# A scan and a feed-forward layer on one core: one wide warm-up product replaced by 32 products of a single column

## The chip, the core and the metric

The kernel runs on one core of a Trainium2 chip. A core has five instruction streams: TensorE (PE in the profile, with its weight loads shown apart as PEld), VectorE (DVE), ScalarE (ACT), GpSimd (POOL) and SyncE (SP), which here only issues DMAs. They meet through semaphores. The metric is the device time of one execution in microseconds: the median of three executions of the kernel before is 309.92 us (309.73 to 310.04).

## The reference

The first half is a gated linear recurrence (a chunked scan) over 4 batches, 8 heads and 768 steps; the second is a feed-forward layer on its output.

```python
for c in range(nc):                       # chunks of the sequence
    cum = np.cumsum(la, axis=-1)          # la = log(clip(a))
    L = np.exp(cum[:, :, :, None] - cum[:, :, None, :]) * causal
    M = np.einsum('bhin,bhjn->bhij', Cc, Bc) * L
    y[:, :, sl] = M @ xc + (Cc @ state) * np.exp(cum)[..., None]
    state = decay_full * state + sum_j(Bc * xc * decay_from_j)
x = y.transpose(0, 2, 1, 3).reshape(3072, 256)
h = x @ w_in                              # 256 -> 2048
return np.maximum(0.01 * h, h) @ w_out    # 2048 -> 256
```

## The kernel before

The sequence is cut into 16 chunks of 48 steps. For each chunk PE forms the logarithms of the decay (`decay_stack`, L267, or for the first two chunks `decay_mask` and `decay_direct`, L249 and L259), ACT takes their exponent (L291), PE forms the scores of C and B (`scores`, L323), DVE multiplies both (`weigh`, L337), and PE multiplies the result with the values (`chunk_products`, L353: 32 products in float32, each of which the profile shows as two). DVE transposes the new state out of PSUM (`states`, L377), and POOL, ACT and DVE copy it in pieces of 16 partitions to where the next chunk reads it (L388). The cumulative sums that most chunks need are made once, by `sums` (L211), from the logarithms of `a`; ACT and DVE split them in three bfloat16 parts, which go through a scratch tensor in memory.

The feed-forward layer runs over tiles of 512 tokens and 16 blocks of 128 hidden features. `ffn_in` (L503) is six products of 512 columns, `ffn_out` (L527) another six; ACT and DVE split what lies between them into a high and a low part (L510, L513, L516). The weights arrive in float64 and are decoded on the way by ACT, DVE and POOL (`decode`, L426 to L472). Later tiles go in pairs through a scheme with fewer products (`two_tiles`, L771 and L796).

The order of the work is written out by hand: each engine runs its instructions in the order in which the code names them. First come constants, the sums and chunks 0 to 2, then a loop over steps, in which one block of the feed-forward layer stands between the pieces of a chunk.

Before any data has arrived, PE runs products on a tile of zeros, `idle`, whose results nobody reads. The helper is `keep_warm` (L118 to L124): each call of it makes `n` products of a 128x128 weight tile with 512 columns. At the start `n` is `WARM`; they write to the second bank of the tile `first`, whose real use begins with `sums`, later on PE's own stream. Between steps 0 and 1 of the loop four more stand (`BRIDGE`).

The lines around the change:

```python
first = banks()
keep_warm(first[:, 1], WARM)
```

Of the kernel before, what the change touches and what calls it, by code (L numbers as in the profile page):

```python
# [29 lines left out]
TS = 512  # L30
LAG = 3
OUT_AT = {1: 0, 2: 1, 3: 2, 4: 3, 5: 4, 8: 5}
WARM = 4
BRIDGE = {1: 4}
RAWS = 3
SLOTS = 2
# [27 lines left out]
def scan_ffn(ctx: ExitStack, tc: tile.TileContext, a_l, c_l, d_l, x_l, w_l, out_l):  # L64
    nc = tc.nc
# [21 lines left out]
    def banks():  # L87
        return ps_c.tile([128, 2, TS], F32, name="sc")
# [26 lines left out]
    idle = const.tile([128, 944], BF16, name="idle")  # L115
    nc.vector.memset(idle[:, :128], 0.0)

    def keep_warm(space, n):  # L118
        for _ in range(n):
            nc.tensor.matmul(  # L120
                space, lhsT=idle[:, :128],
                rhs=idle[:, :128].unsqueeze(1).to_broadcast([128, TS // 128, 128]),
                start=True, stop=True,
            )  # L124

    nc.scalar.preload_act_table_set("natural_log_exp_and_others")
    first = banks()
    keep_warm(first[:, 1], WARM)

    la = pe.tile([128, NC * NM], F32, name="la")  # L130
    nc.sync.dma_start(la, a_l)
# [603 lines left out]
    rhs = {}  # L735
# [318 lines left out]
```

## Time and profile before

| what | before |
| --- | --- |
| median of 3 executions | 309.92 us (309.73 to 310.04) |
| the profiled execution's own time | 309.52 us |
| its span, first to last instruction | 307.5 us |
| PE busy, share of the span | 297.2 us, 97% |
| DVE, ACT, POOL busy | 219.2, 181.8, 72.0 us |
| memory read and written | 20.02 and 3.44 MB |

The span begins with the first instruction and ends with the last; 2.0 us of the execution lie around it. A busy share is an average over the whole span: the first 45 us, where the scan starts up and weights are decoded, look different from the rest. In the rows of a timeline the first number is the start in us, the second the time from there to the end of the last instruction of the row, and x is how many instructions a row holds; in brackets stands how long the engine was idle before it, and what ended that.

### The profile page before, as it was taken

Reading aid. Unit: us, or ns where it says so; the run is one execution under the profiler, and the core shown is the slowest. Engines: PE = TensorE matmul, PEld = TensorE weight load, DVE = VectorE, ACT = ScalarE, POOL = GpSimd, SP = SyncE. Lnnn points to the kernel's source line nnn. Section 1 sums busy time; section 2 is a strip of 40 time slices with the busy share of each in tenths; the row PEclk is TensorE's granted clock in tenths of the full one; section 3 lists DMA queues with packets and bytes.
Section 4 is the critical chain, followed back from the end, with each engine's and each line's share of the span. In section 5 each row is a group of like instructions: output and inputs, shape, how many; then the busy total and the mean of one; then the engine's idle time right before and its main releaser. Section 6 shows DMA issues by size and latency. Waiting matters only on the chain.

```text
span 307.5 us, 6801 instructions
## 1 busy us (share of the span) xinstructions
PE 297.2 (97%) x2712; PEld 234.8 (76%) x2712; DVE 219.2 (71%) x392; ACT 181.8 (59%) x344; POOL 72.0 (23%) x154
## 2 busy tenths in 40 slices
PE   8796999999999999999999999999999999999994
PEld 4464777777777777888888888888888888888883
DVE  6778787987786679975878777776775475547552
ACT  7877566766766554755456565674565455545452
POOL 5444866866676630000000000000000000000000
PEclk9958899999999999999999999999999999999998
DMA  7777764656643101000100000000020000000003
GB/s 238 218 253 237 264 183 158 224 195 220 186 125 112 63 2 71 0 2 0 68 1 2 0 0 0 2 1 0 2 102 34 0 2 1 0 0 2 0 0 136
DMA packets 12644, 23.89 MB, mean 78 GB/s; under 512 B 4549, under 2 KB 4933, under 8 KB 12613
## 3 DMA queue, kind: packets, MB, share of 16 engines
q1 hardware_dynamic: 12612, 23.46, 23.3%
q8 instruction: 21, 0.34, 0.4%
q14 instruction: 11, 0.08, 0.1%
HBM read 20.02 MB, written 3.44 MB: 76 GB/s over the span
## 4 chain that ended last, share of the span: by engine, by line
PE 92%; DVE 3%; issue 2%; ACT 1%; POOL 0%; POOLq 0%; DVEq 0%
PE sc L771 18%; PE op L527 15%; PE op L796 14%; PE sc L796 14%; PE hp L503 14%; PE hp L771 7%; PE sc L353 4%; PE sc L323 3%; PE sc L267 2%; PE sc L120 1%; DVE top L449 1%; PE pd L353 1%; DVE lt L337 1%; DVE gl L516 0%; DVE stage L377 0%
## 5 line engine op out<-in xcount | busy, mean ns | idle before, releaser
L388 POOL COPY xs<-stage 16x128 f32<-16x128 f32 x106 | 37.5, 354 | 26.0 <-DVE stage L377 20.7
L510 ACT ACTIVATE gh<-hp 128x512 fp32r<-128x512 f32 x32 | 19.1, 598 | 28.6 <-PE hp L503 28.4
L807 ACT ACTIVATE gh<-u 128x512 fp32r<-128x512 f32 x32 | 20.0, 625 | 17.7 <-DVE u L848 17.7
L527 PE MATMUL op<-gh,wh 128*128 128x512 f32 x64 | 28.4, 444 | 0.0
L811 DVE TENSOR_TENSOR gl<-u,gh 128x512 fp32r<-128x512 f32 x32 | 22.0, 686 | 7.9 <-ACT u L808 7.9
L847 DVE TENSOR_TENSOR u<-sc,kept 128x512 f32<-128x512 f32 x16 | 11.1, 692 | 22.2 <-PE sc L771 22.2
L807 ACT ACTIVATE gh<-kept 128x512 fp32r<-128x512 f32 x16 | 10.1, 632 | 28.1 <-DVE kept L856 28.1
L527 PE MATMUL op<-gl,wh 128*128 128x512 f32 x64 | 25.6, 399 | 0.1
L527 PE MATMUL op<-gh,wl 128*128 128x512 f32 x64 | 25.5, 399 | 0.0
L807 ACT ACTIVATE gh<-hp 128x512 fp32r<-128x512 f32 x16 | 9.6, 598 | 26.8 <-PE hp L771 26.8
L856 DVE TENSOR_TENSOR kept<-sc,kept 128x512 f32<-128x512 f32 x16 | 11.1, 692 | 19.5 <-PE sc L771 19.3
L796 PE MATMUL op<-gh,wh 128*128 128x512 f32 x64 | 24.9, 389 | 0.0
L796 PE MATMUL sc<-gh,wh 128*128 128x512 f32 x64 | 24.9, 389 | 0.0
L796 PE MATMUL sc<-gh,wl 128*128 128x512 f32 x64 | 24.9, 389 | 0.0
L796 PE MATMUL op<-gh,wl 128*128 128x512 f32 x64 | 24.9, 389 | 0.0
L796 PE MATMUL op<-gl,wh 128*128 128x512 f32 x64 | 24.9, 389 | 0.0
L796 PE MATMUL sc<-gl,wh 128*128 128x512 f32 x64 | 24.9, 389 | 0.0
L337 DVE TENSOR_TENSOR lt<-sc,lt 128x384 f32<-128x384 f32 x32 | 16.3, 549 | 11.3 <-ACT gh L510 8.1
L516 DVE TENSOR_TENSOR gl<-hp,gh 128x512 fp32r<-128x512 f32 x32 | 21.6, 676 | 3.1 <-ACT hp L513 3.1
L472 POOL TENSOR_TENSOR wl<-w,wh 128x512 fp32r<-128x512 f32 x16 | 20.7, 1294 | 11.4 <-ACT wh L471 11.2
L503 PE MATMUL hp<-xh,wh 128*128 128x512 f32 x64 | 20.9, 408 | 0.0
L808 ACT ACTIVATE u<-u 128x512 f32<-128x512 f32 x32 | 20.2, 632 | 1.0
(150 smaller groups left out, 737.8 us busy)
## 6 DMA issues: line engine op xcount, KB each, us to landing
raw<-w_l SPq DMA_DIRECT2D x16, 512.0 KB, 3.8
bcn<-d_l SPq DMA_DIRECT2D x13, 448.0 KB
xs<-x_l SPq DMA_DIRECT2D x16, 256.0 KB, 3.0
out_l<-ob SPq DMA_DIRECT2D x12, 256.0 KB, 2.0
bcn<-c_l SPq DMA_DIRECT2D x3, 352.0 KB
dl<-left_d SPq DMA_DIRECT2D x14, 9.0 KB, 1.6
dr<-right_d SPq DMA_DIRECT2D x14, 9.0 KB
left_d<-parts SPq DMA_DIRECT2D x2, 72.0 KB, 2.4
```

What stands on the lines that cost most here:

```text
L337: nc.vector.tensor_tensor(out=to, in0=at, in1=to, op=ALU.mult)
L388: copy(xss[c + 1][h * R:h * R + N, 2 * p:2 * p + 2, bs], stage[rows, :, bs],)
L472: nc.gpsimd.tensor_tensor(out=wl[:, f], in0=w32s[f], in1=wh[:, f], op=ALU.subtract)
L503: nc.tensor.matmul(hp, lhsT=w_half[h][:, f, k * 128:(k + 1) * 128], rhs=x[t][:, k, :], start=(n == 0), stop=(n == 5),)
L510: nc.scalar.activation(ghs[s], hp, AF.Prelu, alpha=0.01)
L516: nc.vector.tensor_tensor(out=gls[s], in0=hps.pop(s), in1=ghs[s], op=ALU.subtract)
L527: nc.tensor.matmul(op, lhsT=w_half[h][:, f, DM + m * 128:DM + (m + 1) * 128], rhs=x, start=(start and i == 0), stop=(last and i == 2),)
L771: nc.tensor.matmul(bank, lhsT=w[h], rhs=x[g], start=start and i == 0, stop=i == 2, skip_group_check=True,)
L796: nc.tensor.matmul(outs[t][m], lhsT=w_half[h][:, f, DM + m * 128:DM + (m + 1) * 128], rhs=x, start=start and i == 0, stop=last and i == 2,)
L807: nc.scalar.activation(gh, h, AF.Prelu, alpha=0.01)
L808: nc.scalar.activation(in_place, h, AF.Prelu, alpha=0.01)
L811: nc.vector.tensor_tensor(out=gl, in0=g, in1=gh, op=ALU.subtract)
```

## The change

`WARM` goes from 4 to 3, and behind the three wide products stand 32 products of one row of weights, one column of weights and one column of data. They read the same zeros and write one element of the same bank. Nothing else is edited.

```diff
-WARM = 4
+WARM = 3
+NARROW = 32
...
     first = banks()
     keep_warm(first[:, 1], WARM)
+    for _ in range(NARROW):
+        nc.tensor.matmul(
+            first[:1, 1, :1], lhsT=idle[:1, :1], rhs=idle[:1, :1], start=True, stop=True,
+        )
```

On PE the stream before begins like this; `sc` is the bank written to, `bars` the weights of the first real products, `decay_mask`. Lines of the changed file stand five lower from there on.

```order
L1041 UNCONDITIONAL_BRANCH
L120 LDWEIGHTS idle
L120 MATMUL sc<-idle 128x512
L120 LDWEIGHTS idle
L120 MATMUL sc<-idle 128x512
L120 LDWEIGHTS idle
L120 MATMUL sc<-idle 128x512
L120 LDWEIGHTS idle
L120 MATMUL sc<-idle 128x512
L249 LDWEIGHTS bars
```

In the changed kernel PE's stream has the last of the three wide products, and then the first narrow ones, each with a weight load of its own:

```order
L121 LDWEIGHTS idle
L121 MATMUL sc<-idle 128x512
L131 LDWEIGHTS idle
L131 MATMUL sc<-idle 1x1
L131 LDWEIGHTS idle
```

and where they end, the first real products:

```order
L131 LDWEIGHTS idle
L131 MATMUL sc<-idle 1x1
L254 LDWEIGHTS bars
L254 MATMUL pd<-later,bars 128x384
```

One load and one product are gone, 32 loads and 32 products have come: from L254 on everything on PE stands 62 instructions later in its stream (1190 rows of the order, 1128 before), in the same order as before. The streams of DVE, ACT, POOL and SP hold the same instructions in the same order.

## Rows read from the trace of the kernel before

**Rows 1.** From the page: the engines' busy time and instruction counts, and the span in 40 equal slices (each 7.7 us; the busy share in tenths, and the TensorE clock that was granted, in tenths of full speed).

```profile
PE 297.2 (97%) x2712; PEld 234.8 (76%) x2712; DVE 219.2 (71%) x392; ACT 181.8 (59%) x344; POOL 72.0 (23%) x154
PE   8796999999999999999999999999999999999994
PEclk9958899999999999999999999999999999999998
```

**Rows 2.** Timeline of PE, from the start of the span to 13.4 us.

```profile
1.06 1.89 PE L120 MATMUL sc<-idle 128*128 128x512 bf16 x4 [1.06 <-DVE idle L116]
2.74 1.49 PE L249 MATMUL pd<-later,bars 112*128 112x384 bf16 x4
4.02 1.01 PE L211 MATMUL sc<-ends_at,la 112*128 112x96 f32 x4
...
6.13 0.89 PE L323 MATMUL sc<-cs,bcn 32*64 32x96 f32 x32 [0.18 <-ACT cs L302]
6.95 0.30 PE L587 MATMUL sc<-la,after 48*64 48x16 f32 x8
7.09 1.01 PE L259 MATMUL pd<-reach,after 48*64 48x384 f32 x8
8.28 0.86 PE L353 MATMUL pd<-lt,xs 64*32 64x64 f32 x64 [0.19 <-POOL lt L308]
...
10.91 1.41 PE L353 MATMUL sc<-lt,xs 64*32 64x64 f32 x51 [0.31 <-POOL xs L388]
13.09 0.34 PE L353 MATMUL sc<-lt,xs 64*32 64x64 f32 x13 [0.77 <-issue]
```

**Rows 3.** Timeline: the weight loads of L211 on PEld, and ACT's logarithms, whose results L211 reads.

```profile
3.14 0.60 ACT L568 ACTIVATE la<-la 128x32 f32<-128x32 f32 x2
...
3.81 0.29 PEld L211 LDWEIGHTS sc<-ends_at,la 112*128 112x128 f32 x1 [0.28 <-issue]
```

**Rows 4.** Timeline of PE, from 13.3 us on.

```profile
13.36 0.50 PE L267 MATMUL pd<-dr,dl 102*128 102x384 bf16 x2
13.79 0.89 PE L323 MATMUL sc<-cs,bcn 32*64 32x96 f32 x32
15.48 1.74 PE L353 MATMUL pd<-lt,xs 64*32 64x64 f32 x64 [0.80 <-POOL xs L388]
17.15 0.82 PE L267 MATMUL sc<-dr,dl 102*128 102x384 bf16 x2
17.90 0.90 PE L323 MATMUL sc<-bcn 32*64 32x96 f32 x12
19.03 1.22 PE L323 MATMUL sc<-bcn 32*64 32x96 f32 x20 [0.23 <-issue]
20.19 1.22 PE L503 MATMUL hp<-xh,wh 128*128 128x512 f32 x2
21.21 1.05 PE L503 MATMUL hp<-xl,wh 128*128 128x512 f32 x2
22.06 0.74 PE L503 MATMUL hp<-xh,wl 128*128 128x512 f32 x2
22.64 0.50 PE L267 MATMUL sc<-dr,dl 102*128 102x384 bf16 x2
22.98 1.03 PE L120 MATMUL hp<-idle 128*128 128x512 bf16 x4
23.66 0.81 PE L503 MATMUL hp<-xh,wh 128*128 128x512 f32 x2
24.31 0.62 PE L503 MATMUL hp<-xl,wh 128*128 128x512 f32 x2
24.77 0.63 PE L503 MATMUL hp<-xh,wl 128*128 128x512 f32 x2
25.34 0.86 PE L353 MATMUL sc<-lt,xs 64*32 64x64 f32 x64
26.12 0.72 PE L323 MATMUL sc<-bcn 32*64 32x96 f32 x24
29.32 0.60 PE L323 MATMUL sc<-bcn 32*64 32x96 f32 x8 [2.48 <-issue]
```

**Rows 5.** From the page: one of the DMA queues (packets, megabytes, share of the 16 engines' time).

```profile
q8 instruction: 21, 0.34, 0.4%
```

**Rows 6.** Timeline of DVE around the first of PE's stops, and of ACT and DVE after the third.

```profile
13.17 0.30 DVE L443 TENSOR_SCALAR mag<-mag 128x512 uint16<-128x512 uint16 x1
13.51 0.45 DVE L377 STREAM_TRANSPOSE stage<-sc 128x256 f32<-128x256 f32 x1
...
34.16 0.60 ACT L510 ACTIVATE gh<-hp 128x512 fp32r<-128x512 f32 x1 [2.74 <-PE hp L503]
...
36.09 0.29 DVE L438 TENSOR_SCALAR mag<-mag 128x512 bf16<-128x512 bf16 x1 [1.78 <-ACT mag L426]
```

**Rows 7.** The table of busy time by stretches: stretch, its length, busy time of PE, PEld, DVE, ACT and POOL with the number of instructions, the granted clock of TensorE, the DMA engines' share and GB/s.

```profile
15.49:18.90 3.41, 3.19 (x78) 1.89 (x78) 3.30 (x9) 3.31 (x9) 0.38 (x1) 0.50 0.79 284
18.90:22.32 3.42, 3.29 (x25) 2.68 (x26) 2.15 (x5) 1.43 (x5) 3.23 (x6) 0.50 0.72 200
22.32:25.70 3.38, 3.38 (x51) 2.06 (x51) 2.52 (x5) 3.30 (x7) 1.48 (x2) 1.00 0.62 189
25.73:29.14 3.41, 1.12 (x65) 0.90 (x55) 3.27 (x6) 2.29 (x5) 1.99 (x2) 1.00 0.95 304
29.14:32.56 3.42, 3.23 (x14) 2.45 (x14) 3.38 (x8) 1.10 (x2) 2.09 (x4) 0.50 0.77 241
```

## The prediction

> **What bounds the kernel now.** I read the slices of the page first. PE is busy in nine tenths or more of every slice but three early ones and the last, so a microsecond that PE loses before about 45 us is lost for good, unless another engine was late at that place anyway [rows 1]. Then I read PE's timeline through that early part, row by row, looking at the brackets. Two things are to be seen there.
>
> The first is the start. The four wide products run from 1.06 us, the first real ones (L249) from 2.74, so a wide one takes 1.68 / 4 = 0.42 us, and the four L249, from 2.74 to 4.02, 0.32 us each [rows 2]. 512 columns in 0.42 us and 384 in 0.32 are both 1.2 GHz, the lower of the clock's two levels. Behind them stands L211. Its weights are the logarithms, which ACT finishes at 3.14 + 0.60 = 3.74 us, and its weight load starts at 3.81 [rows 3]; its product starts at 4.02, just where the last L249 ends. So PE's own work and the logarithms come due at nearly the same time. A PE that is later than now delays L211 in full; one that is earlier gains at most 0.2 us. Everything of the scan hangs on L211, since ACT's next work reads it.
>
> The second is three places where PE is idle and the bracket names "issue": no semaphore and no engine ended the wait. They are 0.77 us inside a group of L353 after its 51st product of 64, 0.23 us inside a group of L323 after the 12th of 32, and 2.48 us inside another group of L323 after the 24th of 32 [rows 2, 4]. Nothing in the code stands at these places. Counted along PE's rows, 13 + 2 + 32 + 64 + 2 + 12 = 125 products lie between the first stop and the second, and 20 + 6 + 2 + 4 + 6 + 64 + 24 = 126 between the second and the third [rows 4]. With a weight load for each and a few semaphore waits that is about 256 instructions both times. The DMA queue q8 carried instructions: 21 packets with 0.34 MB, 16 KB each [rows 5]; PE's 2712 products and 2712 loads [rows 1] divided by 21 are 258 instructions a packet. I take the three stops for refills of PE's instruction store that came too late, one at each border of 256 instructions, in a stretch where DMAs keep their engines 62 to 95% busy [rows 7].
>
> [...]
>
> **The change part by part.** Durations are those of the profiled execution (309.52 us, span 307.5 with 2.0 around it); it lies 0.40 below the median of 309.92, and I add the sum to the median.
>
> *One wide product goes:* -0.42 us.
>
> *32 narrow ones come.* No row shows a product of one column. From below, the rows of L353 at 8.28 bound it: 64 products with 64 loads in 0.86 us, 13 ns each, or 0.43 us for 32. These lie on different parts of the array, and narrow ones all on the same. From above, a narrow one could wait for its own weight load each time; the nearest load that stands alone is L211's, 0.29 us for 128 columns in float32 [rows 3], or 9.3 us for 32. That is far off, since in L353 64 loads pass in 0.86 us. Nearer are L587, the shortest stream of data here (16 columns), with 8 in 0.30 us, 37 ns each or 1.20 us, and L323, with 32 in 0.89, 28 ns each [rows 2]. I take L323, whose count is that of the change: 0.89 us. The two parts together are +0.47 us, between 0 and +0.8 by the near rows, and it lies in full on the way to L211. The lower end is not below nothing by more than the 0.2 us that L211 could gain.
>
> [...]
>
> *The borders move.* 31 more products and 31 more loads stand ahead of everything, so each border falls 31 products earlier in the program: the first after the 20th of the 64 products of L353 (about 11.7 us on the old clock), the second after the 47th of the group of L353 at 15.48 (about 16.6), the third after the 57th of the group at 25.34 (about 26.0) [rows 2, 4]. I assume that a refill is asked for when the border before it is crossed, since the time from one restart to the next landing is what varies; that crossing is now earlier too: 11.7 in place of 13.09 for the second and 16.6 in place of 19.03 for the third. For the third, the time from one border to the next grows from 29.32 - 2.48 - 19.03 = 7.8 to 9.4 us; for the second it shrinks from 5.7 (18.80 - 13.09) to 4.9. I forecast that the stops mostly go.
>
> What that is worth: the first stop is hidden. DVE was busy until 13.17 + 0.30 = 13.47 and took its transpose at 13.51, 0.02 us after PE's last product, so PE could have been earlier for nothing [rows 6]. The second is worth its 0.23 us. The third is 2.48 us on PE; ACT waited 2.74 us for the L503 behind it, but DVE, which is busy 3.27 and 3.38 of 3.4 us in the two stretches beside it, waited only 1.78 us at 36.09 [rows 6, 7]. So DVE is next late, and 1.78 us is what comes through. Together -2.01 us.
>
> *The clock* was halved from 15.49 to 22.32 and from 29.14 to 32.56; PE was busy 1.12 us of 3.41 ahead of the second [rows 7]. Without the third stop that second stretch may be at full speed, worth up to half of its 3.23 busy us, 1.6; or PE, now waiting for DVE a little later, makes it fall later, and loses as much. I take 0 and keep both for the range.
>
> Sum: -0.42 + 0.89 - 2.01 = -1.54 us, so 309.92 - 1.54 = 308.4 us. By the ends (0 and +0.8 for the narrow ones, -1.6 for the clock) this case runs from 309.92 - 2.01 - 1.6 = 306.3 to 309.92 - 2.01 + 0.8 = 308.7, and to 309.2 if half a microsecond of stops stays.
>
> **The rivals.**
>
> *The clock rises later.* In the rows of the start PE is at 1.2 GHz; at 6.13 L323 takes 0.89 us for 32 products, the same as at full speed later, where 20 take 1.22 us at half [rows 2, 4]. So the clock rises at about 5 us, behind four microseconds of dense wide products. Now about one of these holds products that fill one cell of the array. From 15.49 to 18.90 PE was busy 3.19 of 3.41 us, mostly with products on small parts of the array, and the clock stayed at 0.50 after it [rows 7]. Against it speaks that three wide ones, L249 and L211 stay. If the clock stays low until about 10 us, a group of scores goes from 26 ns a product (6.13 to 6.95 for 32) to 58 (19.03 to 20.19 for 20), +1.0 us for 32, and a group of L353 from 0.86 to about 1.5, +0.6. Two groups of scores and one of L353 on the way make +2.6 us, and with the forecast's other terms 311.0 us. It decides from 1.5 us of added time on. [...]
>
> *The narrow ones are dear.* If load and product took turns on the one place of the array, at 0.10 us a pair (a third of L211's load alone), 32 would cost 3.2 us. Then 3.2 - 0.42 - 2.01 = +0.8, 310.7 us. Against it: loads in L353 pass at 13 ns [rows 2].
>
> *The refills take as long as before.* From crossing to restart the second took 19.03 - 13.09 = 5.9 us and the third 29.32 - 19.03 = 10.3. With these, the second lands at 11.7 + 5.9 = 17.6, a stop of 1 us in place of 0.23, and the third at 27.9, 1.4 before the old one, but with 7 products of L353 and 24 of L323 still to run, 0.8 us. The gain left is about 0.5 us and the narrow ones eat it: 309.9 us. For it speaks that a refill's time seems set by the DMAs around it; against it, that those DMAs are not the same ones at the earlier crossings.
>
> [...]
>
> **How the numbers follow.** The forecast has 0.42, the later clock 0.22, dear narrow ones 0.14, refills as slow as before 0.14, no refills 0.08. About 0.2%, 0.6 us, is what a measurement of this kernel can tell from no change: faster means under 309.3, slower over 310.5. The forecast is faster (0.42, and 0.01 from refills half as slow); slow refills and no refills fall within (0.21 of their 0.22); the two first rivals are slower, 0.36. The forecast's own range is 306.3 to 309.2; its low end needs the whole gain of the clock, so the range with both signs begins at 307.0, and it ends at 311.6, above both slower cases by half a microsecond.
>
> **What would show it.** In PE's timeline of the changed kernel the first L254 starts at 2.32 + 0.89 = 3.2 us and L216 (the old L211) at about 4.5. The "issue" brackets, if any are left, stand 31 products earlier in the program, and the waits named "issue" before the scores sum to under 1 us. The scores at about 6.6 us take 0.89 us if the clock has risen, near 1.9 if not. ACT's wait for L508 (the old L503) near 34 us is shorter than 2.74. The forecast is wrong if a stop of over 1 us stands inside a group of L358 or L328, if the first real product starts after 4 us, or if the granted clock is low at 7 us.

## The result, and the profile after

The changed kernel is slower: 311.42 us (median of 20, 309.63 to 312.68), and the kernel before, run beside it, 309.55 (20, 308.28 to 311.04). The ratio is 1.006, 95% interval 1.004 to 1.008. The forecast was 308.4.

One thing must be known to read the profile after. Its execution took 309.63 us, the shortest of the 20. A second profile of the same kernel, taken in the first experiment, took 311.35, close to the median. I call them the short and the typical execution and use both.

From the page of the short execution, the lines that answer to [rows 1] and [rows 5]:

```profile
PE 296.1 (96%) x2743; PEld 232.7 (76%) x2743; DVE 221.0 (72%) x392; ACT 181.7 (59%) x344; POOL 72.5 (24%) x154
...
PE   8978789999999999999999999999999999999994
...
PEclk9999999999999999999999999999999999999999
...
q8 instruction: 21, 0.34, 0.4%
```

31 more products, as many packets on q8 (21). PE's timeline of the short execution, the start, against [rows 2], and the places where PE waits later, against [rows 4]:

```profile
1.06 1.46 PE L121 MATMUL sc<-idle 128*128 128x512 bf16 x3 [1.06 <-DVE idle L117]
2.45 0.94 PE L131 MATMUL sc<-idle 1*1 1x1 bf16 x32
3.32 1.46 PE L254 MATMUL pd<-later,bars 112*128 112x384 bf16 x4
4.57 1.01 PE L216 MATMUL sc<-ends_at,la 112*128 112x96 f32 x4
...
7.00 1.56 PE L328 MATMUL sc<-cs,bcn 32*64 32x96 f32 x32
...
13.02 1.21 PE L358 MATMUL sc<-lt,xs 64*32 64x64 f32 x64 [0.31 <-POOL xs L393]
...
32.55 0.48 PE L272 MATMUL sc<-dr,dl 102*128 102x384 bf16 x2 [1.76 <-issue]
...
41.83 0.48 PE L272 MATMUL sc<-dr,dl 102*128 102x384 bf16 x2 [1.11 <-issue]
```

The narrow products start 25 ns apart (32 lie between 2.45 and 3.25); from the first of them to L254 it is 0.87 us, and L216 starts 0.55 us later than L211 did. The three stops inside L353 and L323 are gone. But the scores at 7.00 take 1.56 us where they took 0.89: the records of the granted clock begin, at full, only at 10.91 us, before at 5.25 (the slices of the page show the time ahead of the first record as full). And two new waits stand before L272, which the view also calls "issue"; the rows of DVE below show what is late there.

The typical execution, same view:

```profile
13.72 1.19 PE L358 MATMUL sc<-lt,xs 64*32 64x64 f32 x64 [0.32 <-DMA dl<-left_d]
...
17.47 0.78 PE L358 MATMUL pd<-lt,xs 64*32 64x64 f32 x46 [0.24 <-DVE lt L342]
19.71 0.47 PE L358 MATMUL pd<-lt,xs 64*32 64x64 f32 x16 [1.47 <-issue]
20.11 0.82 PE L272 MATMUL sc<-dr,dl 102*128 102x384 bf16 x2
20.87 1.55 PE L328 MATMUL sc<-bcn 32*64 32x96 f32 x32
22.35 1.22 PE L508 MATMUL hp<-xh,wh 128*128 128x512 f32 x2
...
34.31 0.48 PE L272 MATMUL sc<-dr,dl 102*128 102x384 bf16 x2 [1.38 <-issue]
43.59 0.48 PE L272 MATMUL sc<-dr,dl 102*128 102x384 bf16 x2 [1.10 <-issue]
```

Here the second stop is back: 1.47 us, behind the 48th of 64 products (2 + 46) of the L358 group, where the prediction's count put the border (the 47th). The table of stretches of the same execution, against [rows 7]:

```profile
18.90:22.32 3.42, 2.60 (x50) 1.62 (x50) 1.78 (x6) 2.02 (x7) 0.83 (x1) 0.57 0.15 41
25.73:29.14 3.41, 3.41 (x79) 2.24 (x77) 3.10 (x6) 2.73 (x7) 1.08 (x1) 0.93 0.73 231
```

Behind the stop the clock is down (0.57 in the mean) and the loads are through (DMA share 0.15). In the second stretch PE is busy 3.41 of 3.41 us, where the third stop had left 1.12.

**Where the time went.** Two rows of DVE cut the execution into three parts: M is the L438 (after: L443) behind its wait for ACT near 24 us, P the transpose L377 (L382) near 46. In the kernel before they are

```profile
23.62 0.97 DVE L438 TENSOR_SCALAR mag<-mag 128x512 bf16<-128x512 bf16 x1 [0.79 <-ACT mag L426]
...
46.29 0.45 DVE L377 STREAM_TRANSPOSE stage<-sc 128x256 f32<-128x256 f32 x1 [1.22 <-PE sc L353]
```

In the typical execution of the changed kernel (timeline of DVE and POOL):

```profile
25.91 1.05 DVE L443 TENSOR_SCALAR mag<-mag 128x512 bf16<-128x512 bf16 x1 [0.78 <-ACT mag L431]
...
33.22 0.98 DVE L342 TENSOR_TENSOR lt<-sc,lt 128x384 f32<-128x384 f32 x2
...
39.03 3.04 POOL L477 TENSOR_TENSOR wl<-w,wh 128x512 fp32r<-128x512 f32 x2
...
39.54 1.38 DVE L443 TENSOR_SCALAR mag<-mag 128x512 bf16<-128x512 bf16 x1
40.95 1.26 DVE L448 TENSOR_SCALAR mag<-mag 128x512 uint16<-128x512 uint16 x1
...
42.51 0.98 DVE L342 TENSOR_TENSOR lt<-sc,lt 128x384 f32<-128x384 f32 x2
...
48.06 0.45 DVE L382 STREAM_TRANSPOSE stage<-sc 128x256 f32<-128x256 f32 x1 [1.16 <-PE sc L358]
```

Both L342 end (34.20 and 43.49) 0.1 us before the L272 that waited (34.31 and 43.59): PE waits there for DVE. Up to M it loses 25.91 - 23.62 = 2.29 us. From M to P it takes 22.15 in place of 22.67, a gain of 0.52. From P to the end of the time it is 311.35 - 48.06 = 263.29 against 309.52 - 46.29 = 263.23. In all 20 profiles of this study this last part lies between 263.2 and 263.6 us. So everything is decided before P, and the loss lies ahead of M.

In the typical execution the chain that ended last leads from the second stop to M: the 1.47 us of the stop, the rest of L358, L272, the scores L328 until 22.47, then L342, L454 and L463 on DVE, L476 and L431 on ACT, and M. The start of L508, which stands behind the scores on PE, is used below as the mark of their end.

### The profile page after: what moved, and what is told of

It is laid out like the page before. It is cut to its first block, busy times and chain, and to the rows that moved or that the text cites. A ratio compares the mean times of both kernels' runs of the same rounds, so it can differ in the third digit from the quotient of the medians.

```text
span 307.6 us, 6863 instructions
## 1 busy us (share of the span) xinstructions
PE 296.1 (96%) x2743; PEld 232.7 (76%) x2743; DVE 221.0 (72%) x392; ACT 181.7 (59%) x344; POOL 72.5 (24%) x154
## 3 DMA queue, kind: packets, MB, share of 16 engines
q1 hardware_dynamic: 12612, 23.46, 23.5%
## 4 chain that ended last, share of the span: by engine, by line
PE 87%; DVE 5%; DMA 4%; SPq 1%; issue 1%; ACT 0%; DVEq 0%
PE sc L776 18%; PE op L801 14%; PE sc L801 14%; PE op L532 14%; PE hp L508 13%; PE hp L776 7%; PE sc L358 3%; PE sc L328 2%; DMA bcn<-d_l 2%; PE sc L272 1%; DMA left_d<-parts 1%; DVE top L454 1%; DVE w L463 1%; DMA dr<-right_d 1%; DVE gl L521 1%
## 5 line engine op out<-in xcount | busy, mean ns | idle before, releaser
L393 POOL COPY xs<-stage 16x128 f32<-16x128 f32 x106 | 36.9, 349 | 27.6 <-DVE stage L382 22.2
L342 DVE TENSOR_TENSOR lt<-sc,lt 128x384 f32<-128x384 f32 x32 | 16.3, 549 | 11.1 <-ACT gh L515 8.3
L477 POOL TENSOR_TENSOR wl<-w,wh 128x512 fp32r<-128x512 f32 x16 | 21.1, 1326 | 7.3 <-ACT wh L476 7.0
L508 PE MATMUL hp<-xh,wh 128*128 128x512 f32 x64 | 20.3, 398 | 0.3 <-ACT wh L476 0.3
```

What stands on the lines that cost most here:

```text
L342: nc.vector.tensor_tensor(out=to, in0=at, in1=to, op=ALU.mult)
L393: copy(xss[c + 1][h * R:h * R + N, 2 * p:2 * p + 2, bs], stage[rows, :, bs],)
L477: nc.gpsimd.tensor_tensor(out=wl[:, f], in0=w32s[f], in1=wh[:, f], op=ALU.subtract)
L508: nc.tensor.matmul(hp, lhsT=w_half[h][:, f, k * 128:(k + 1) * 128], rhs=x[t][:, k, :], start=(n == 0), stop=(n == 5),)
```

## The experiments

Ratios are to the kernel before, run beside each, with the 95% interval. Times of refills are the starts of the 16 KB packets on q8 in the trace's DMA records. "Clock" is the time from which the records grant it in full.

**The changed kernel again, and the kernel before again** (no edit).

> The changed kernel once more, for a second profile of it, since its times spread by 3 us and the profile there is one of its fastest executions. All theories: 310.5 to 312 us. Theory D (the code refill that now comes at 8.5 us holds up the save of the sums, left_d, on which SP's queue waits): left_d lands 3.5 us or more after its issue again, the refill's packet lies beside it. Theory C (the clock rises later behind the narrow products): the granted clock rises after 7 us again. Theory F (refills still come too late in most executions): stops named issue of over 1 us stand in PE's timeline 31 products earlier than before.

> The kernel before once more, for a second profile of it. Theory C: the clock rises near 5 us again. Theory R (the refill stops are part of this kernel in every execution): stops named issue inside the same three groups, after the 51st, 12th and 24th product, 2 to 4 us together; if they are shorter here, their length is set by the DMAs of one execution.

The changed kernel: 311.49, ratio 1.0085 (1.0067 to 1.0103), the typical execution above. The kernel before: 309.18, ratio 1.0014 (0.9990 to 1.0038); in its profile the clock happened to rise as late as in the changed kernel, at 13.05 us. That execution took 309.63, 0.45 over the median of its own 12 runs. PE's timeline and M and P of DVE's:

```profile
13.25 1.18 PE L353 MATMUL sc<-lt,xs 64*32 64x64 f32 x64
...
18.26 0.55 PE L323 MATMUL sc<-bcn 32*64 32x96 f32 x12
19.66 0.71 PE L323 MATMUL sc<-bcn 32*64 32x96 f32 x20 [0.85 <-issue]
20.30 0.73 PE L503 MATMUL hp<-xh,wh 128*128 128x512 f32 x2
...
23.96 1.08 DVE L438 TENSOR_SCALAR mag<-mag 128x512 bf16<-128x512 bf16 x1 [0.78 <-ACT mag L426]
...
46.34 0.45 DVE L377 STREAM_TRANSPOSE stage<-sc 128x256 f32<-128x256 f32 x1 [1.22 <-PE sc L353]
```

This is the pair to look at. Second packet at 17.35 here, 17.41 in the typical execution of the changed kernel; PE goes on at 19.66 here, 19.71 there. The refill is equally late. But here PE stands behind the 12th of 32 scores and reaches the feed-forward product 0.64 us later; there 16 products of L358, L272 and all 32 scores are still to come, 2.64 us at the half clock that follows the stop.

**The wide products alone**: `WARM = 5`, `WARM = 3`, `WARM = 0`, no narrow ones; the borders stay within ten instructions of where they were.

> Five wide products at the start and no narrow ones: PE reaches the first real product 0.43 us later, nearly what the change does (0.57), with a dense start and the refill borders where they were. If delay alone is the cause (theory L) the time rises by 0.4 us or more, towards what the change costs. Theories C and D: like the kernel before, within 0.5 us; refills, left_d and the clock's rise (near 5 us) as before.

> Three wide products and no narrow ones: the other half of the edit alone, without the moved borders. Theory C in the form that a wide product is missed: the clock rises later than before and the time goes up by 1 us or more. Theory D: the same as before, or up to 0.2 us faster, with left_d landing 2.4 us after its issue as before.

> No product before the first real ones at all: PE begins near 2.4 us. No narrow products, borders moved by 8 instructions only, and no delay. Theory C prices the late clock alone: it rises after 8.5 us, and the time is 2 to 3 us over the kernel before, about that of the change. If delay, borders or collision are the cause of the change's loss, this kernel is within 0.5 us of the kernel before.

Medians 309.73, 309.78, 309.30; ratios 1.0012 (0.9984 to 1.0039), 1.0026 (1.0002 to 1.0050), 1.0018 (0.9992 to 1.0044). The clock rose at 5.51 with five, at 12.79 with three and at 12.60 with none. Without any warm-up the kernel can't be told from the one before, and the 2 to 3 us that theory C gave for e11 are out: a late clock with the old borders costs little or nothing (only the interval of e3 stays clear of 1, by 0.0002).

**The borders moved, with the start as before.** 31 narrow products later in PE's stream, behind the four wide ones: behind the first `decay_direct` (e12) or behind the `reverse` products L597 (e4, e10, the same kernel twice).

```
+        for _ in range(31):
+            nc.tensor.matmul(
+                pd[:1, 0, :1], lhsT=idle[:1, :1], rhs=idle[:1, :1], start=True, stop=True,
+            )
         states(0, os, (0, 0, 0, 2, 0, 2, 0, 2))
```

> Four wide products as before, and 31 narrow ones behind the two products of L597, where PE waits for the copies of the state anyway. The start is that of the kernel before, but every refill border behind the first falls 31 products earlier, as in the change. Theory D: the first refill is asked for as before, left_d lands as before (2.4 us), the stops at 12, 19 and 27 us shrink, and the time is 0.5 to 2 us under the kernel before. Theory F: the moved borders are what costs, and the time is above the kernel before by 1 us or more. Theory C: as before or faster.

> e4 once more, for a second profile and more times. Theory C: clock up near 5 us. Theory R: the third stop is gone again, but by 45 us PE is at most 1 us ahead of the kernel before, since DVE is the bound from 20 to 41 us; the time is within 0.4% of the kernel before.

> Four wide products as before; 31 narrow ones behind the first group of L259, just ahead of the first scores, where PE waits 0.2 us for ACT. All borders, the first one too, fall 31 products earlier as in the change, and the scores come about 0.6 us later, but the start up to L211 is that of the kernel before. Theory C: the clock rises near 5 us, and the time is within 0.7 us of the kernel before. Theories D and F (collision, borders): 1 us or more over the kernel before, like the change; by D, left_d lands 3.5 us or more after its issue.

310.21, 310.51 and 309.74; ratios 1.0033 (1.0013 to 1.0053), 1.0039 (1.0015 to 1.0062), 1.0023 (0.9998 to 1.0049). The clock rose at 4.7 to 4.9 us in all three. So this edit with an early clock costs 0.7 to 1.2 us by these ratios, about half of the loss; e12's interval includes no cost. It is not the borders alone: in e4 the 31 narrow products take 0.84 us on PE, where it waited 0.31 us before, and the group of L353 behind them starts at 11.37 in place of 10.91. How the cost divides between this delay and the borders was not tested, and the profiles don't show where it arises, since all three are of executions under the median of their runs (308.96, 309.66, 308.58). In e12 the save of `left_d` landed 3.9 us after its issue, as in the short execution (4.0; before 2.4): that delay, which I had suspected at first, does not by itself make an execution slow.

**Order and mixture.** e5: the 32 narrow products ahead of the three wide ones. e6: four wide, then 32 narrow. e8: three wide, and the 31 behind L597.

```
-    keep_warm(first[:, 1], WARM)
     for _ in range(NARROW):
...
         )
+    keep_warm(first[:, 1], WARM)
```

> The change with its two parts in the other order: the 32 narrow products first, then the three wide ones, then the first real products. Instructions, borders, delay (0.57 us) are those of the change; only the dense products now follow on each other without a break. Theory C (the narrow products between dense ones keep the clock low): it rises near 6 us, and the time is 1 us or more under the change, near 310 us. Theories D, F and L (collision, borders, delay): the same time as the change, 311 to 312 us.

> Four wide products and then the 32 narrow ones: the narrow ones are added and nothing is taken away. Theory C, if it is the narrow stretch that counts: the clock still rises late, 311.5 us or more. If it is the wide product that is missed: the clock rises near 6 us and the time lies near 310 us. Theories D, F, L: 0.4 us over the change (PE is another wide product later).

> Three wide products, and 31 narrow ones only behind L597, where PE waits anyway: the edits of e3 and e4 together, with the instruction count of the change. If the change is no more than the sum of a missing wide product (+0.26% in e3) and moved borders (+0.33% in e4), this is 0.6% over the kernel before, as slow as the change. Theory C with the narrow stretch at the start as the cause: clearly under the change, at most 0.4% over the kernel before.

e6 is as slow as the change, though no wide product is missing: 312.06, ratio 1.0095 (1.0063 to 1.0126), clock at 13.68, a stop of 1.42 us. e5 holds the same work as the change in another order: 309.72, 1.0043 (1.0016 to 1.0069), clock at 4.83. Its median is 1.7 us under the change's, but by the ratios the gain is 0.5 to 1.3 us, and the intervals overlap. Its times lie in two clusters, 308.3 to 309.9 and 310.6 to 311.8. e8: 310.74, 1.0056 (1.0033 to 1.0078), clock at 10.06, a stop of 1.97 us. That is the plain sum which it was to test (e3's 0.26% and e4's 0.33%), so the narrow products need not stand at the start for the loss. In the profiles the clock is late (10.06 to 15.24 us) wherever the narrow ones are the last of the warm-up or fewer than four wide ones stand in it without narrow ones ahead; of nine profiles with four or five wide ones last, one (e9) had it late (13.05).

**What lies ahead of the second refill.** SP issues three loads at about the time at which PE crosses the first moved border, after the 20th product of the L358 group. SP's DMA issues (`raw`, `bcn`, `xs` of a later chunk) in the typical execution, with the border at 13.72 + 20 x 1.12 / 64 = 14.07 us:

```profile
12.57 0.35 SPq L97 DMA_DIRECT2D raw<-w_l  x1
13.02 0.38 SPq L106 DMA_DIRECT2D bcn<-d_l  x1
13.49 0.38 SPq L114 DMA_DIRECT2D xs<-x_l  x1
```

and in the short one, with the border at 13.02 + 20 x 1.22 / 64 = 13.40:

```profile
13.37 0.35 SPq L97 DMA_DIRECT2D raw<-w_l  x1
13.82 0.38 SPq L106 DMA_DIRECT2D bcn<-d_l  x1
14.29 1.73 SPq L114 DMA_DIRECT2D xs<-x_l  x1
```

The view of the DMA queues shows the refill of the short execution in a window from 14.0 to 15.5 us, and that of the typical one from 17.0 to 18.5:

```profile
q8 instruction: 1, 0.02, 5.1%
```

```profile
q8 instruction: 1, 0.02, 4.3%
```

The loads are no news, though: in the kernel before, SP issues the same three at 11.28, 12.21 and 12.69 us. PE crosses the border there when its first stop ends, at 13.09, and the packet starts 3.5 us later; in the typical execution of the changed kernel the first product behind the border starts at 14.23 in the records, and the packet 3.2 us later. So the time from border to packet has not grown; PE crosses the border 1.1 us later. Over all 20 profiles, the packet starts 2.6 to 3.7 us after that product in the twelve with the loads where they were and `raw` and `bcn` issued before it. It starts 0.9, 1.2 and 1.9 us after it in three with `bcn` issued after it (short, e12, e19), but 2.9 us after it in a fourth (e4), so the order of issue is not the whole of it.

So the 448 KB load of `bcn` was moved behind the refill, in the changed kernel (e13), in the kernel before (e14), in e5 (e15) and in e4 (e16):

```
         fetch_w(1)
-        fetch_c(3)
...
         load_rows(4)
+        fetch_c(3)
```

> The changed kernel with one load moved: the 448 KB bcn<-d_l load of chunk 3 is issued on SP after the rows of chunk 4 instead of before them, so that less lies ahead of the second instruction refill (packet seen at 14.4 us in the fastest run of the change, at 17.4 to 17.8 us in the runs with 311.4 and 311.7 us). Theory (the second refill lies behind the loads): the second packet starts about 2 us earlier, 15.5 us or before, TensorE's stop inside L358 is under 0.5 us even where the clock rises only after 10 us, and the time is 309.5 to 310.5 us, 1 us or more under the change. Rival (the late clock, or the place of the border, costs by itself): the median stays at 311 to 312 us.

> The kernel before with the same load moved. Theory: the second refill packet (16.6 us in the profile of before) starts at 14.5 to 15.5 us and the second stop (1.78 us or 0.85 us) is gone; since VectorE bounds the stretch to 41 us, the time is the same or up to 1 us under the kernel before. Rival (the load is needed early: scores of chunk 3 wait for it): 0.5 to 2 us slower, with a wait of L328 on bcn<-d_l.

> The 32 narrow products first, then 3 wide ones, with the load moved. Without the move the times lay in two clusters, about 308.3 to 309.9 us and 310.6 to 311.8 us. Theory: the upper cluster is the late second refill, and it goes: median 308.5 to 309.3 us, all runs under 310.3 us. Rival (the upper cluster is the clock alone): two clusters as before, median 309.5 to 310 us.

> 4 wide products, and 31 narrow ones behind the first L597, with the load moved. Without the move: medians 310.2 and 310.5 us, second packet at 15.1 and 15.9 us. Theory: second packet at 13.5 to 14.5 us, no stop over 0.5 us before 25 us, median 308.3 to 309.3 us. Rival (the narrow products' own delay and the borders' place cost by themselves): 310 to 310.5 us as before.

e13: 310.58, ratio 1.0050 (1.0026 to 1.0074). The median is 0.84 below the change's, nearer to the theory than to the rival's 311 to 312; by the ratios (1.0059 and 1.0085 for the change) the gain is 0.3 to 1.1 us, and the intervals overlap. The trace is clearer: the packet came at 16.27, 1.1 us earlier, though not before 15.5, and the stop shrank by 1.1, with the clock still late (13.31):

```profile
18.68 0.35 PE L358 MATMUL pd<-lt,xs 64*32 64x64 f32 x16 [0.36 <-issue]
```

e14: 309.71, 1.0006 (0.9977 to 1.0034). The packet came at 15.84, 0.75 us earlier and not by 15.5. The second stop went and the rival's wait came in its place, so it tells nothing of the stop's price:

```profile
19.05 1.56 PE L323 MATMUL sc<-bcn 32*64 32x96 f32 x32 [2.20 <-DMA bcn<-d_l]
```

e15: 310.24, 1.0020 (0.9991 to 1.0049): a miss, though its packet came at 14.16 (e5 14.55); the upper cluster of e5 is still there (310.6 to 311.3), so it isn't made by this load. e16: 309.88, 1.0018 (0.9992 to 1.0044), 0.3 to 0.6 under e4 and e10, but above the 309.3 that the theory allowed, and not to be told from them by the intervals. Its theory failed in the trace too: the packet came at 15.48, between those of e4 and e10 (15.07 and 15.85), and the stop is 1.14 us.

**What the third stop was worth.** Four of the eight copies L393 behind chunk 3 given to ACT, in the change (e17), the kernel before (e18) and e5 (e19):

```
-            states(c, os)
+            states(c, os, (0, 2, 0, 2, 0, 2, 0, 2) if c == 3 else (2,) * 8)
```

> The changed kernel, with four of the eight POOL copies of L393 behind chunk 3 given to ACT (1.77 of 3.54 us less on POOL near 35 to 38 us). Theory (what the third stop's removal freed on VectorE is taken again by VectorE operations that wait for POOL): POOL's two L477 no longer run back to back, VectorE's L443 and L448 beside them go from 1.38 and 1.26 us to near 0.29 each, the stretch from VectorE's wait for L431 near 24 to 26 us to its wait before L382 near 46 to 48 us shrinks from 22.1 - 22.4 us to about 20.3, and the median falls by 1 to 2 us, to 309.4 to 310.4 us. Rival (these durations have nothing to do with POOL, or the length of this stretch is set elsewhere): the stretch stays at 22.1 to 22.6 us and the median at 311 us or more.

> The same four copies given to ACT in the kernel before. Theory: here VectorE waits for the third stop (1.4 to 1.8 us before L438), so only the 1.06 us that L449 takes over its usual 0.75 us can go; the stretch shrinks by under 1 us, and the median falls by 0 to 1 us, to 308.4 to 309.5 us: less than the changed kernel gains by the same edit. Rival: no difference, or ACT's four copies make it up to 1 us slower.

> The 32 narrow products first, then 3 wide ones (median 309.7 us, with runs at 308.3 to 309.9 and at 310.6 to 311.8 us), with the same four copies given to ACT. Theory: no third stop and no stretch beside POOL, so 1 to 2 us faster than without: median 307.7 to 308.7 us, which would be under both kernels. Rival: 309.5 us or more, as without.

312.32, 309.53 and 311.39; ratios 1.0079 (1.0048 to 1.0109), 0.9993 (0.9969 to 1.0018), 1.0054 (1.0028 to 1.0080). Right in the small and wrong in the sum. In e17 POOL's two L477 no longer run back to back, and L443 and L448 are at 0.29 us again (timeline of DVE and POOL):

```profile
35.75 0.56 DVE L412 TENSOR_TENSOR xl<-sc,xh 128x384 fp32r<-128x384 f32 x1 [0.96 <-ACT xh L404]
...
39.18 1.28 POOL L477 TENSOR_TENSOR wl<-w,wh 128x512 fp32r<-128x512 f32 x1 [2.14 <-ACT wh L476]
...
39.50 1.57 DVE L454 SCALAR_TENSOR_TENSOR top<-raw,mag 128x512 uint16<-128x512 uint16 x1
...
41.78 0.29 DVE L443 TENSOR_SCALAR mag<-mag 128x512 bf16<-128x512 bf16 x1
42.10 0.29 DVE L448 TENSOR_SCALAR mag<-mag 128x512 uint16<-128x512 uint16 x1
```

But DVE waits 0.96 us for an ACT that has the copies to do first, and L454, usually 0.75 us, takes 1.57 beside one L477. From M (26.14) to P (48.29) it is 22.15 us, to the hundredth what the typical execution takes. e17's median is 0.8 to 0.9 us above the change's, but its ratio of 1.0079 lies between the change's two (1.0059 and 1.0085), so the edit neither gained nor lost anything that can be told. Its profile has the second packet at 17.81 and a stop of 1.71 us. e18 is as its rival had it, no difference. e19 missed its theory by about 3 us.

## Why the prediction was wrong, step by step

| profile | clock | first moved border | second packet | PE goes on | to L503/L508 | M | M to P | time |
| --- | --- | --- | --- | --- | --- | --- | --- | --- |
| before | 5.25 | 12.32 | 16.59 | 19.03 | 1.16 | 23.62 | 22.67 | 309.52 |
| before again (e9) | 13.05 | 14.14 | 17.35 | 19.66 | 0.64 | 23.96 | 22.38 | 309.63 |
| change, short | 10.91 | 13.40 | 14.44 | no stop | | 23.80 | 22.51 | 309.63 |
| change, typical (e1) | 12.54 | 14.07 | 17.41 | 19.71 | 2.64 | 25.91 | 22.15 | 311.35 |
| change, load moved (e13) | 13.31 | 14.15 | 16.27 | 18.68 | 1.59 | 24.46 | 22.53 | 310.62 |

(The border stands after the 51st product of the group in the kernel before, after the 20th in the changed one. Its time is spread evenly over the group, for the first row the end of the 51st product. By the records of single products the first one behind the border starts at 13.09, 14.09, 13.54, 14.23 and 14.31, from top to bottom.)

*The edits themselves* were right. +0.47 us was forecast, +0.55 at L216 came; the narrow ones and what follows them up to L254 take 0.87 us where I took 0.89, and the last wide one ends a little later than forecast. The rival of dear narrow products (3.2 us) is out.

*That the stops are refills, and stand 31 products earlier*, was right. Wherever PE stops at one of the first two borders, in any of the 20 profiles, it goes on 2.2 to 2.8 us after a packet starts on q8, and in the changed kernel the stops stand where the count puts them, to one product. That the stops are no refills, to which the forecast gave 0.08, is out. One reading is off and changes nothing: DVE's transpose at 13.51 starts 0.08 us behind PE's last product (13.43), not 0.02.

*"That crossing is now earlier too: 11.7 in place of 13.09"* is the first step that failed. The border is earlier in the program, but PE reaches it later: 0.55 us for the edits and more for the late clock put it at 14.07. The loads of SP are ahead of it as they were in the kernel before, the packet starts at 17.41, and the stop that was to go (0.23 us) is 1.47. Up to M the forecast had +0.47 for the edits and -0.23 for this stop, +0.24 together; +2.29 came: PE goes on 0.68 later (19.71 against 19.03), needs 2.64 in place of 1.16 us to the feed-forward product (+1.48), and 3.56 in place of 3.43 from there to M (+0.13). Of the 1.48 the place of the border is the larger part: at full clock e13 needs 1.59 from there and e9, with the old border, 0.64, a difference of 0.95.

*"1.78 us is what comes through"* of the third stop is the other step that failed. The stop went, as forecast, and 0.52 us came through (22.67 to 22.15), or 0.16 in the short execution. "DVE is next late" was right, but DVE's own time was not fixed: L443 and L448 beside POOL's two L477 take 1.38 + 1.26 in place of 0.58, 2.06 us more. The kernel before had paid a part of that already, in another operation: behind its wait of 1.78 us, L449 takes 1.81 in place of 0.75 beside one L472 of POOL.

```profile
37.16 1.29 POOL L472 TENSOR_TENSOR wl<-w,wh 128x512 fp32r<-128x512 f32 x1 [0.96 <-ACT wh L471]
37.23 1.81 DVE L449 SCALAR_TENSOR_TENSOR top<-raw,mag 128x512 uint16<-128x512 uint16 x1
```

So 1.00 us net of the freed 1.78 is given back there, and small differences elsewhere take the remaining 0.78 down to 0.52. Against the second profile of the kernel before (e9, 22.38, with a third stop of 2.12) only 0.23 came through. e14, which lost the third stop with the old borders, takes 46.10 - 23.91 = 22.19 too. Whichever wait is taken away there, the stretch comes out at 21.8 to 22.7 us, except in e3 and e19, 24.0: a further stop of 1.60 us lies in it in e3 (at 39.84), and 6.8 us at the half clock in e19 (33.29 to 40.12).

*The clock rises later* was the rival whose sign of the profile came true, scores of 1.56 us at 7.00. But its sum was wrong in kind. It priced the slow products one by one, +2.6 us; e9, e11 and e3 have the same late clock with the old borders at ratios of 1.0014 to 1.0026, under 0.8 us. In the traces of the changed kernel it makes PE cross the border late, and through that the refill. *The refills take as long as before* was nearest to what happened at the second stop: from the crossing to the restart it is 19.71 - 14.23 = 5.5 us, where the kernel before took 5.9. It gave a stop of 1 us in place of 0.23, and would have been slower and not the same had it not credited the third stop with half a microsecond and taken the crossing at 11.7. By the ratios, the old borders with a late clock cost 0.4 to 0.8 us (e9, e11, e3), moved borders with an early clock 0.7 to 1.3 (e12, e4, e10, e5), and both 1.7 to 2.9 (e8, the change, e6). The first two add up to 1.1 to 2.1, so the times don't show whether the two make each other dearer; the pair of e9 and the typical execution shows one way in which they can.

In the one profile of e13, with a load less ahead of the refill, M is 1.45 us earlier (25.91 to 24.46), and the clock, which halves at 19.37 in the typical execution, stays up; so the queue ahead of the refill is a part of the cause as far as one profile can tell. What stays open: why the clock rises late with the narrow products last; the rest of the loss, since M is still 0.84 above the kernel before there; how much of that 1.45 reaches the median; and why executions of one kernel differ by up to 3 us. That difference lies ahead of M too, in the pairs of profiles that show one (23.80 and 25.91 for the change, 23.46 and 24.18 for e4 and e10, 0.70 us apart in time). No version that was tried beats the kernel before: e18 at 0.9993 can't be told from it.

## What to carry to other kernels

A product that nobody reads is still a load and a product in PE's stream (31 more of each here), and moved every later border: the second stop went from behind the 12th of 32 scores to behind the 48th of 64 products of L358. Count it as a change of place, not only of time. When a stop goes away, add up what the next engine does with the time before crediting it: durations of DVE beside POOL were not constants here (L443 took 0.29 and 1.38 us). And a small delay upstream can grow at a refill: between the short and the typical execution PE crosses the border 0.7 us later (13.54 and 14.23), and the packet starts 3.0 us later (14.44 and 17.41; 16.27 with the 448 KB load of `bcn` issued later, in e13).

## What the runs showed of the hardware that was not expected

- A weight load with a product of one row and one column passes in 25 ns (32 in 0.80 us) ahead of the first clock record, about what a score takes at the full clock (28 ns). Wide products start 0.43 us apart there, 1.2 columns per ns, which the prediction calls 1.2 GHz; the four wide ones between the steps, with the clock recorded at 1.00 (21.9 to 22.6 us of the short execution), start 0.22 us apart, half of that. The records of both kernels hold no level but 1.00 and 0.50.
- A refill of PE's, as these stops were read, is one packet of 16 KB (21 with 0.34 MB on q8) and about 1 us (0.9 to 1.6 where PE used it in the first 45 us). In the two rows of the pair above PE went on 1.3 us behind its end (17.41 + 1.02 = 18.43, then 19.71; 17.35 + 0.99 = 18.34, then 19.66).
- DVE's TENSOR_SCALAR of 0.29 us ended 1.38 and 1.26 us after its start where two POOL operations of 1.52 us ran beside it, and L454 took 1.57 in place of 0.75 beside one. Why they take longer there no run shows; the delays are 1.1, 1.0 and 0.8 us, none longer than the one POOL operation of 1.52 or 1.28 us.
- The same three wide and 32 narrow products gave an early clock with the narrow ones first (4.83, 6.14 and 5.98 us in e5, e15 and e19) and a late one with them last (10.91 to 15.24 in four profiles). The clock of one kernel is not fixed either: the kernel before had it at 5.25 us in one profile and at 13.05 in the other.
